# Keeping the MLP pre-activation in bf16 and taking SiLU's slope from one later ScalarE pass

## Chip, cores and metric

One core of a Trainium2 (trn2) chip. The metric is device time in microseconds (us), lower is better.

## The reference, cut to what matters

Two long-convolution blocks `A` and two MLP blocks `B` alternate with residual adds; the outputs are the result and the gradients of all inputs and weights, from one call.

```python
def _B_ref(x, w1, w2):                       # x 2048x448, w1 448x1792, w2 1792x448, all bf16
    h = jnp.einsum("bsd,df->bsf", x, w1)
    h = _silu(h)
    return jnp.einsum("bsf,fd->bsd", h, w2)

x = x + _A_ref(_layernorm(x), k, v, ...)
x = x + _B_ref(_layernorm(x), B_w1, B_w2)    # "layer 0"
x = x + _A_ref(_layernorm(x), k, v, ...)
x = x + _B_ref(_layernorm(x), B_w1, B_w2)    # "layer 1"
# outputs: x and the vjp with grad_out for q, k, v, shift_k, ssm_k, ssm_D, w1, w2
```

The backward of `silu` needs its slope at every one of 2048 x 1792 pre-activations, in both layers.

## The kernel before

The kernel has three parts: a spectral prefix for `A` (to about 107 us), the MLP part (to about 555 us), and a suffix with the backward of `A` and the weight gradients. The MLP part walks over the sequence in four chunks of 512. For each chunk and layer, `h` computes the 1792 hidden features in two halves of seven 128-row tiles; two PSUM buffers `ps_h` take the matmul results in turn.

```python
def h(self, c, L, nT, half, hold):
    aT = self.td.tile([P, NF // 2, 512], BF16, name="aT", tag="T", bufs=3)
    dT = self.td.tile([P, NF // 2, 512], BF16, name="dT", tag="D", bufs=3)
    hold.append((aT, dT))
    for ft0, n in ((0, 2), (2, 2), (4, 2), (6, 1)) if half == 0 else ((7, 1), (8, 2), (10, 2), (12, 2)):
        ps = k.psum.tile([P, 2, 512], FP32, name="ps_h", tag="mm", bufs=2)
        ...                                                       # 4 or 8 matmuls into ps
        nc.scalar.activation(a, ps[:, 0:n, :], ACT.Silu)                      # L543
        nc.scalar.activation(tm, ps[:, 0:n, :], ACT.Tanh, scale=-0.5)         # L544
        wv = ...                                                  # tile w1p, bufs=1
        nc.vector.tensor_scalar(out=wv, in0=tm, scalar1=1.0, scalar2=None, op0=ALU.add)   # L547
        nc.vector.tensor_tensor(out=wv, in0=wv, in1=a, op=ALU.mult)                       # L548
        nc.vector.tensor_tensor(out=tm, in0=wv, in1=tm, op=ALU.subtract)                  # L549
    if L == 1:
        ...                                     # dT = Copy(dT, bias=1.0), four ScalarE pieces
    else:
        nc.gpsimd.dma_start(out=k.DT_d[c, half], in_=dT[:])       # to memory; load_l0 adds the 1.0 later
```

With t = tanh(-x/2), twice the slope is 1 - t + (1 + t) * silu(x); the three VectorE operations form it without the 1, and `rh` (half of `rstd`) takes the factor 2 out again. Other users of VectorE in these loops are the residual adds (`X`), the layer norm's statistics (`ln_st`, `ln_mv`), and the backward reductions `ln_bwd`. VectorE works through one queue, in order: in its timeline, shown below, a slope operation (L548, at 175.13 us) starts only as the 2.02 us residual add that was queued ahead of it (L514, at 173.19 us) ends.

In the suffix, `_wgrad_w2_first` reads activations back with transposing loads, `dstat<-A_d` on SyncE's queue, while GpSimd's queue fetches other large tiles:

```python
        _load_minv(k, nc.gpsimd)                                  # Minvs, 1 MB
        ...                                                       # fft stage 1
        _wgrad_w2_first(k, None, range(10, NF))                   # last transposed loads dstat<-A_d
        ...
            nc.gpsimd.dma_start(out=t[0], in_=k.SPEC_d["K"][:, lo:hi])        # kk_c, 0.5 MB each
            nc.gpsimd.dma_start(out=t[1], in_=k.SPEC_d["KV"][:, lo:hi])
            if cp == 2:
                nc.gpsimd.dma_start(out=ksf[:], in_=_pm(k.KS_d[:]))           # 1.8 MB
```

Of the kernel before, what the change touches and what calls it, by code (L numbers as in the profile page):

```python
# [10 lines left out]
FP32 = mybir.dt.float32  # L11
BF16 = mybir.dt.bfloat16
ACT = mybir.ActivationFunctionType
# [4 lines left out]
P = 128  # L18
S = 2048
D = 448  # L20
# [100 lines left out]
def kernel(  # L121
# [52 lines left out]
    k.Gsb = keep.tile([P, 5, P], BF16, name="Gsb")  # L174
    nc.gpsimd.dma_start(out=k.Gsb[:].rearrange("p a k -> p (a k)"), in_=gs_h.ap())
    k.rstd = [keep.tile([P, J], FP32, name=f"rstd{i}") for i in range(4)]
    k.rh = [keep.tile([P, J], FP32, name=f"rhalf{i}") for i in range(2)]
    k.mhalf = keep.tile([P, 4], FP32, name="mhalf")
    nc.gpsimd.memset(k.mhalf[:], -0.5)
    nc.scalar.activation(k.rh[1][:, 0:4], k.mhalf[:], ACT.Silu)  # L180
    k.wk = ctx.enter_context(tc.tile_pool(name="wk", bufs=1))
    k.dp = ctx.enter_context(tc.tile_pool(name="dp", bufs=1))
    with tc.tile_pool(name="yk", bufs=1, side="right") as yk:
# [275 lines left out]
class Main:  # L459
# [64 lines left out]
    def b_tr(self, n_g):  # L524
        nT = self.ch.tile([P, ND, 512], BF16, name="nT", tag="nT", bufs=2)
        self.transp(n_g, nT, [(DC * i, DC * i + DC) for i in range(4)])
        return nT

    def h(self, c, L, nT, half, hold):
        nc, k = self.nc, self.k  # L530
        aT = self.td.tile([P, NF // 2, 512], BF16, name="aT", tag="T", bufs=3)
# [4 lines that stand above are left out]
            for u in range(n):  # L536
                ft = ft0 + u
                for dc in range(ND):
                    nc.tensor.matmul(ps[:, u, :], lhsT=self.w1sb[:, dc, ft * P:(ft + 1) * P], rhs=nT[:DC, dc, :], start=(dc == 0), stop=(dc == ND - 1))  # L539
            o = ft0 - 7 * half  # L540
            a = aT[:, o:o + n, :]
            tm = dT[:, o:o + n, :]
            nc.scalar.activation(a, ps[:, 0:n, :], ACT.Silu)  # L543
            nc.scalar.activation(tm, ps[:, 0:n, :], ACT.Tanh, scale=-0.5)  # L544
            w = self.ch.tile([P, 2, 512], BF16, name="w1p", tag="w1p", bufs=1)
            wv = w[:, 0:n, :]
            nc.vector.tensor_scalar(out=wv, in0=tm, scalar1=1.0, scalar2=None, op0=ALU.add)  # L547
            nc.vector.tensor_tensor(out=wv, in0=wv, in1=a, op=ALU.mult)  # L548
            nc.vector.tensor_tensor(out=tm, in0=wv, in1=tm, op=ALU.subtract)  # L549
            k.bal.add("act", 1.05 * n)  # L550
            k.bal.add("dve", 0.9 * n)
        if L == 1:
            for o in range(0, 7, 2):
                n = min(2, 7 - o)
                nc.scalar.activation(dT[:, o:o + n, :], dT[:, o:o + n, :], ACT.Copy, bias=1.0)
            k.bal.add("act", 3.4)
        else:
            nc.gpsimd.dma_start(out=k.DT_d[c, half], in_=dT[:])
            self.store_plain(k.A_d[0], aT, c, half)
        if L == 1:  # L560
            self.store_turned(k.A_d[1], aT, c, half)
# [54 lines left out]

    def ln_bwd(self, u0, n_t, cp, g_res, G_out):
        nc = self.nc
        junk = self.ch.tile([P, D], BF16, name="lb_junk", tag="w1p", bufs=1)
        nc.vector.scalar_tensor_tensor(out=junk[:], in0=u0, scalar=1.0, in1=n_t, op0=ALU.mult, op1=ALU.mult, accum_out=cp[:, 1:2])  # L620
        cc = self.ch.tile([P, 2], FP32, name="lb_cc", tag="lb_cc", bufs=2)
        nc.vector.tensor_scalar(out=cc[:], in0=cp, scalar1=-1.0 / D, scalar2=None, op0=ALU.mult)
        nc.vector.scalar_tensor_tensor(out=u0, in0=n_t, scalar=cc[:, 1:2], in1=u0, op0=ALU.mult, op1=ALU.add)  # L623
        nc.vector.scalar_tensor_tensor(out=G_out, in0=u0, scalar=cc[:, 0:1], in1=g_res, op0=ALU.add, op1=ALU.add)  # L624
        self.k.bal.add("dve", 2.0)

    def gn(self, c, L, ghT, nb, gres, na):
# [7 lines left out]
        for tl in range(4):  # L635
            t = 4 * c + tl
            pn = k.psum.tile([P, 512], FP32, name="ps_n", tag="tr" if L == 1 and tl % 2 else "po", bufs=2)
            for ft in range(NF):
                nc.tensor.matmul(pn[:, :D], lhsT=ghT[ft // 7][:, ft % 7, tl * P:(tl + 1) * P], rhs=self.w1T[:, ft, :], start=(ft == 0), stop=(ft == NF - 1))  # L639
            u0 = self.ch.tile([P, D], FP32, name="lb_u0", tag="lb_u0", bufs=2)  # L640
            nc.scalar.activation(u0[:], pn[:, :D], ACT.Identity, scale=k.rh[L][:, t:t + 1], accum_out=cp[:, tl, 0:1])
            k.bal.add("act", 0.75)
            self.ln_bwd(u0[:], nb[:, tl, :], cp[:, tl, :], gres(tl), G[:, t, :])
            if L == 1:
                nc.vector.tensor_tensor(out=gyt[:, tl, :], in0=G[:, t, :], in1=na[:, tl, :], op=ALU.mult)
            else:
                gy = self.ch.tile([P, D], FP32, name="gy", tag="lb_u0", bufs=2)
                nc.vector.tensor_tensor(out=gy[:], in0=G[:, t, :], in1=na[:, tl, :], op=ALU.mult)
                nc.vector.tensor_tensor(out=k.gYb[:, t, :], in0=gy[:], in1=gyt[:, tl, :], op=ALU.add)
            u1 = self.ch.tile([P, D], FP32, name="lb_u1", tag="lb_u0", bufs=2)  # L650
            nc.vector.scalar_tensor_tensor(out=u1[:], in0=G[:, t, :], scalar=k.rstd[si][:, t:t + 1], in1=self.Y[:, t, :], op0=ALU.mult, op1=ALU.mult, accum_out=cp[:, 4 + tl, 0:1])
            k.bal.add("dve", 1.3)
            self.ln_bwd(u1[:], na[:, tl, :], cp[:, 4 + tl, :], G[:, t, :], G[:, t, :])
# [5 lines left out]
    def load_l0(self, c):  # L659
# [3 lines left out]
        for hh in range(2):  # L663
            t = self.td.tile([P, NF // 2, 512], BF16, name="dTl", tag="D", bufs=3)
            i = nc.sync.dma_start(out=t[:], in_=k.DT_d[c, hh])
            if c == 0:
                k.d0_load = i
            for o in range(0, 7, 2):
                n = min(2, 7 - o)
                nc.scalar.activation(t[:, o:o + n, :], t[:, o:o + n, :], ACT.Copy, bias=1.0)  # L670
            k.bal.add("act", 3.2)
            dT.append((None, t))
        nb = self.ch.tile([P, 4, D], BF16, name="nb_l", tag="nb", bufs=2)
        nc.sync.dma_start(out=nb[:], in_=_pm(k.N_d[1][:])[:, sl, :])
# [14 lines left out]
    def run(self):  # L689
# [7 lines left out]
        for c in range(4):  # L697
# [10 lines left out]
            self.h((c + 1) % 4, 0 if c < 3 else 1, nT, 0, fol)  # L708
            self.out(c, cur, False)
            cur = fol  # L710
        nc.vector.tensor_scalar(out=k.rh[0][:], in0=k.rstd[1][:], scalar1=0.5, scalar2=None, op0=ALU.mult)
        for c in range(4):
            gb, gT = self.g_pre(c, 1)
            self.h(c, 1, nT, 1, cur)
            if c < 3:
                na1 = self.a_fwd(c + 1, 2, None)
            nc.vector.tensor_scalar(out=k.rh[1][:, 4 * c:4 * c + 4], in0=k.rstd[3][:, 4 * c:4 * c + 4], scalar1=0.5, scalar2=None, op0=ALU.mult)
            self.out(c, cur, True)
            box = []
            ghT = self.ga(c, 1, gT, cur, (lambda: box.append(self.b_pre(c + 1, 3))) if c < 3 else None)  # L720
# [67 lines left out]
def _wgrad_rest(k, pool, after, mov3):  # L788
# [13 lines left out]
    def fin_w1(ft, ps, aux):  # L802
# [3 lines left out]
        for dc in range(ND):  # L806
            nc.tensor.transpose(pt[:, dc, :], o[:, dc * DC:(dc + 1) * DC], k.ident[:])  # L807
        o7 = pool.tile([DC, ND, P], BF16, name="do7", tag="do7", bufs=2)
        nc.scalar.activation(o7[:], pt[:], ACT.Copy, scale=0.5)  # L809
        nc.gpsimd.dma_start(out=out7v[:, :, ft * P:(ft + 1) * P], in_=o7[:])  # L810

    with k.tc.issue_after(after[-1]):
# [191 lines left out]
```

## Time and profile before

| | before |
|---|---|
| three runs known at the prediction, us | 869.88, 869.68, 858.88 |
| span of the profiled execution | 868.2 us |
| MLP part: first SiLU / first output cast / fourth output cast / last `ps_n` group starts at | 112.03 / 242.22 / 407.98 / 555.57 us |

Those four marks are found in every trace, and the three stretches between them are compared. The first holds all of layer 0's forward and the first chunk's forward in layer 1 (five chunk steps), the second three full chunk steps of layer 1, the third the last backward chunk of layer 1 and layer 0's backward. The stretch table of the kernel before (columns: window, its length, busy us of PE, PEld, DVE, ACT and POOL with counts, granted clock, DMA share, GB/s):

```profile
112.03:242.22 130.19, 122.41 (x639) 57.74 (x638) 112.35 (x253) 107.29 (x135) 33.88 (x39) 1.00 0.61 199
242.22:407.98 165.76, 153.98 (x793) 73.66 (x792) 129.86 (x294) 120.44 (x151) 20.09 (x25) 0.96 0.71 182
```

TensorE (PE) is 94% busy in the first stretch, VectorE (DVE) 86%.

The timeline of VectorE shows how these belong together (start us, duration, engine, line, operation):

```profile
172.99 0.29 DVE L547 TENSOR_SCALAR w1p<-dT 128x512 bf16<-128x512 bf16 x1
173.19 2.02 DVE L514 TENSOR_TENSOR X<-x0c,a_t 128x1792 f32<-128x1792 bf16 x1
175.13 0.42 DVE L548 TENSOR_TENSOR w1p<-w1p,aT 128x512 bf16<-128x512 bf16 x1
175.46 0.62 DVE L256 BATCH_NORM_STATS2 ln_st<-X 128x6 f32<-128x448 f32 x1
176.00 0.41 DVE L549 TENSOR_TENSOR dT<-w1p,dT 128x512 bf16<-128x512 bf16 x1
```

Slope operations and the next chunk's residual add and statistics stand in one queue with no gap, so each slope operation ahead of them pushes back the statistics, and with them the normalization of the next chunk (L270), for which TensorE waited 2.9 us in this stretch.

### The profile page before, as it was taken

How to read it: one execution, taken by the hardware profiler on the slowest of the kernel's cores; microseconds unless marked ns; L12 is line 12 of the kernel's file. 1: busy time of each engine (PE TensorE's matmuls, PEld its weight loads, DVE VectorE, ACT ScalarE, POOL GpSimd, SP SyncE). 2: the span in 40 equal slices, each digit the busy share in tenths (PEclk: the TensorE clock that was granted, in tenths of full speed). 3: DMA queues.
4: the chain of work that ended last, by engine and by line, in shares of the span. 5: the costliest groups of instructions: out<-in, count | busy, mean ns of one | idle time of the engine just before them, and what ended most of it. 6: DMA issues, size and time to landing. Idle time of an engine off the chain costs nothing.

```text
span 868.2 us, 12830 instructions
## 1 busy us (share of the span) xinstructions
PE 755.6 (87%) x4924; PEld 410.3 (47%) x4924; DVE 565.7 (65%) x1201; ACT 481.9 (56%) x598; POOL 145.7 (17%) x218
## 2 busy tenths in 40 slices
PE   6997699999999899897978879993579896989997
PEld 4975434444444344343433334451346564545553
DVE  4789778898938969779387989962166632760100
ACT  5789678787968585788666654232145433330010
POOL 1143222322110120110000101111111121221010
PEclk9999899999999899899989999997799998999999
DMA  9279895455667576596795654999988879987771
GB/s 324 99 234 271 304 261 193 176 207 212 149 175 169 166 176 168 154 245 192 178 254 174 232 153 136 225 257 227 200 293 291 267 276 244 125 231 175 185 186 44
DMA packets 168392, 178.60 MB, mean 206 GB/s; under 512 B 135374, under 2 KB 139086, under 8 KB 167308
## 3 DMA queue, kind: packets, MB, share of 16 engines
q1 hardware_dynamic: 144304, 81.70, 39.6%
q0 software_dynamic: 21696, 88.07, 31.7%
q10 hardware_dynamic: 2332, 8.03, 3.1%
q8 instruction: 38, 0.62, 0.3%
q14 instruction: 22, 0.18, 0.1%
HBM read 66.64 MB, written 70.65 MB: 158 GB/s over the span
## 4 chain that ended last, share of the span: by engine, by line
DVE 25%; DMA 21%; issue 20%; PE 16%; ACT 14%; POOL 4%; ACTq 0%; SPq 0%; POOLq 0%; DVEq 0%
DMA dstat<-A_d 4%; PE ps_d L773 4%; DMA xsw_c<-Zg 3%; DVE lb_u L623 3%; DVE X L624 2%; DMA GY_d<-gyt 2%; DVE lb_junk L620 2%; DMA out_dram<-gKD 2%; PE ps_g L598 2%; DVE dT L549 2%; DVE w1p L548 2%; DVE ghT L607 2%; PE ps_h L539 2%; ACT ghp L602 2%; ACT aT L543 2%
## 5 line engine op out<-in xcount | busy, mean ns | idle before, releaser
L773 PEld LDWEIGHTS <-dstat 128*128 128x128 bf16 x896 | 87.0, 98 | 104.9 <-DMA dstat<-A_d 24.7
L598 PE MATMUL ps_g<-gT,w2T 128*128 128x512 bf16 x448 | 110.8, 398 | 20.3 <-ACT ghp L602 17.1
L773 PE MATMUL ps_d<-mov,dstat 128*128 128x448 bf16 x448 | 95.6, 357 | 23.9 <-DMA dstat<-A_d 23.9
L539 PE MATMUL ps_h<-nT,w1sb 112*128 112x512 bf16 x448 | 106.7, 384 | 6.3 <-ACT dT L544 4.6
L639 PE MATMUL ps_n<-w1T,ghT 128*128 128x448 bf16 x448 | 94.5, 358 | 10.0 <-DVE ghT L607 6.9
L773 PE MATMUL ps_d<-dmov,dstat 128*128 128x448 bf16 x448 | 94.6, 353 | 4.7 <-DMA dmov<-N_d 2.9
L569 PE MATMUL ps_o<-w2sb,aT 128*128 128x448 bf16 x448 | 92.6, 352 | 1.4 <-DVE X L570 1.3
L598 PEld LDWEIGHTS <-w2T 128*128 128x128 bf16 x448 | 45.4, 101 | 78.6 <-issue 33.6
L602 ACT CAST ghp<-ps_g 128x1024 bf16<-128x1024 f32 x56 | 56.4, 1007 | 35.8 <-PE ps_g L598 14.4
L539 PEld LDWEIGHTS <-w1sb 112*128 112x128 bf16 x448 | 43.7, 98 | 62.5 <-issue 18.3
L639 PEld LDWEIGHTS <-ghT 128*128 128x128 bf16 x448 | 43.4, 99 | 56.4 <-DVE ghT L607 11.0
L543 ACT ACTIVATE aT<-ps_h 128x1024 bf16<-128x1024 f32 (+1 forms) x64 | 59.2, 925 | 9.3 <-PE ps_h L539 5.1
L569 PEld LDWEIGHTS <-aT 128*128 128x128 bf16 x448 | 42.5, 98 | 42.5 <-ACT aT L543 3.0
L544 ACT ACTIVATE dT<-ps_h 128x1024 bf16<-128x1024 f32 (+1 forms) x64 | 59.4, 928 | 0.0
L804 DVE CAST dout<-ps_d 128x448 bf16<-128x448 f32 x14 | 8.7, 624 | 75.6 <-PE ps_d L773 75.6
L809 ACT ACTIVATE do<-ps_dt 112x512 bf16<-112x512 bf16 x14 | 8.4, 598 | 74.9 <-PE ps_dt L807 74.9
L228 PE MATMUL ps_v<-Gsb,pa 128*128 128x128 bf16 x336 | 43.7, 223 | 5.5 <-DVE Zg L113 3.2
L229 PE MATMUL ps_v<-Gsb,pb 128*128 128x128 bf16 x336 | 42.6, 223 | 5.3 <-DVE pb L884 2.7
L547 DVE TENSOR_SCALAR w1p<-dT 128x1024 bf16<-128x1024 bf16 (+1 forms) x64 | 26.5, 415 | 23.7 <-ACT dT L544 22.1
L229 PEld LDWEIGHTS <-pb 128*128 128x128 bf16 x336 | 33.0, 100 | 15.5 <-DVE pb L438 6.0
L548 DVE TENSOR_TENSOR w1p<-w1p,aT 128x1024 bf16<-128x1024 bf16 (+1 forms) x64 | 39.6, 619 | 1.0
L549 DVE TENSOR_TENSOR dT<-w1p,dT 128x1024 bf16<-128x1024 bf16 (+1 forms) x64 | 39.5, 618 | 1.0
(184 smaller groups left out, 1311.6 us busy)
## 6 DMA issues: line engine op xcount, KB each, us to landing
A_d<-aT POOLq DMA_DIRECT2D x8, 896.0 KB, 5.5
DT_d<-dT POOLq DMA_DIRECT2D x8, 896.0 KB, 4.2
A_d<-turned POOLq DMA_DIRECT2D x8, 896.0 KB, 4.8
GH_d<-turned POOLq DMA_DIRECT2D x8, 896.0 KB, 7.3
dTl<-DT_d SPq DMA_DIRECT2D x8, 896.0 KB, 6.0
GH_d<-ghT POOLq DMA_DIRECT2D x8, 896.0 KB, 8.2
dstat<-A_d SPq DMA_DIRECT2D x14, 512.0 KB, 6.4
dstat<-GH_d SPq DMA_DIRECT2D x14, 512.0 KB, 3.8
```

The costliest lines, as they stand in the source:

```text
L228: nc.tensor.matmul(pv[:, i, :], lhsT=pa[:, i * P:(i + 1) * P], rhs=k.Gsb[:, ga, :], start=True, stop=False)
L229: nc.tensor.matmul(pv[:, i, :], lhsT=pb[:, i * P:(i + 1) * P], rhs=k.Gsb[:, gb, :], start=False, stop=True)
L539: nc.tensor.matmul(ps[:, u, :], lhsT=self.w1sb[:, dc, ft * P:(ft + 1) * P], rhs=nT[:DC, dc, :], start=(dc == 0), stop=(dc == ND - 1))
L543: nc.scalar.activation(a, ps[:, 0:n, :], ACT.Silu)
L544: nc.scalar.activation(tm, ps[:, 0:n, :], ACT.Tanh, scale=-0.5)
L548: nc.vector.tensor_tensor(out=wv, in0=wv, in1=a, op=ALU.mult)
L549: nc.vector.tensor_tensor(out=tm, in0=wv, in1=tm, op=ALU.subtract)
L569: nc.tensor.matmul(po[:, :D], lhsT=aT[ft // 7][0][:, ft % 7, tl * P:(tl + 1) * P], rhs=self.w2sb[:, ft, :], start=(ft == 0), stop=(ft == N ...
L598: nc.tensor.matmul(ps[:, u, :], lhsT=self.w2T[:, b, ft * P:(ft + 1) * P], rhs=gT[:, b, :], start=(b == 0), stop=(b == ND - 1))
L602: nc.scalar.copy(gh[:], ps[:])
L639: nc.tensor.matmul(pn[:, :D], lhsT=ghT[ft // 7][:, ft % 7, tl * P:(tl + 1) * P], rhs=self.w1T[:, ft, :], start=(ft == 0), stop=(ft == NF - 1))
L773: nc.tensor.matmul(ps[:, :D], lhsT=st[:, t, :], rhs=movs[gi][:, t, :], start=(gi == 0 and t == 0), stop=(gi == len(groups) - 1 and t == NT ...
```

## The change

The intent: do not compute the slope in four steps at the place where SiLU is computed and a fifth one later. Evict the pre-activation x itself to bf16 in the place of Tanh, and apply ScalarE's `Derivative_silu` to it in the later pass that so far only added 1.0. The diff, cut to its core:

```diff
+    def slope(self, d):
+        for o in range(0, 7, 2):
+            n = min(2, 7 - o)
+            self.nc.scalar.activation(d[:, o:o + n, :], d[:, o:o + n, :], ACT.Derivative_silu)
 ...
             nc.scalar.activation(a, ps[:, 0:n, :], ACT.Silu)
-            nc.scalar.activation(tm, ps[:, 0:n, :], ACT.Tanh, scale=-0.5)
-            w = self.ch.tile([P, 2, 512], BF16, name="w1p", tag="w1p", bufs=1)
-            ...                                  # the three VectorE operations
+            e = nc.scalar if o == 4 else nc.vector
+            _copy(nc, e, tm, ps[:, 0:n, :])
         if L == 1:
-            ...                                  # the Copy pass with bias=1.0
+            if half == 1:
+                for _, d in hold:
+                    self.slope(d)
 ...
-        junk = self.ch.tile([P, D], BF16, name="lb_junk", tag="w1p", bufs=1)
+        junk = self.ch.tile([P, D], BF16, name="lb_junk", tag="lb_junk", bufs=1)
 ...                                              # load_l0: Copy pass -> self.slope(t); halved scales undone
```

More of the change, by code (lines that the diff above doesn't have):

```diff
@@ L176 @@
     k.rstd = [keep.tile([P, J], FP32, name=f"rstd{i}") for i in range(4)]
-    k.rh = [keep.tile([P, J], FP32, name=f"rhalf{i}") for i in range(2)]
+    k.warm = keep.tile([P, 4], FP32, name="warm")
     k.mhalf = keep.tile([P, 4], FP32, name="mhalf")
     nc.gpsimd.memset(k.mhalf[:], -0.5)
-    nc.scalar.activation(k.rh[1][:, 0:4], k.mhalf[:], ACT.Silu)
+    nc.scalar.activation(k.warm[:], k.mhalf[:], ACT.Silu)
     k.wk = ctx.enter_context(tc.tile_pool(name="wk", bufs=1))
@@ L527, in b_tr @@
         return nT
+    def slope(self, d):
+        for o in range(0, 7, 2):
+            n = min(2, 7 - o)
+            self.nc.scalar.activation(d[:, o:o + n, :], d[:, o:o + n, :], ACT.Derivative_silu)
+        self.k.bal.add("act", 3.4)
     def h(self, c, L, nT, half, hold):
@@ L543, in h @@
             nc.scalar.activation(a, ps[:, 0:n, :], ACT.Silu)
-            nc.scalar.activation(tm, ps[:, 0:n, :], ACT.Tanh, scale=-0.5)
-            w = self.ch.tile([P, 2, 512], BF16, name="w1p", tag="w1p", bufs=1)
-            wv = w[:, 0:n, :]
-            nc.vector.tensor_scalar(out=wv, in0=tm, scalar1=1.0, scalar2=None, op0=ALU.add)
-            nc.vector.tensor_tensor(out=wv, in0=wv, in1=a, op=ALU.mult)
-            nc.vector.tensor_tensor(out=tm, in0=wv, in1=tm, op=ALU.subtract)
-            k.bal.add("act", 1.05 * n)
-            k.bal.add("dve", 0.9 * n)
+            e = nc.scalar if o == 4 else nc.vector
+            _copy(nc, e, tm, ps[:, 0:n, :])
+            k.bal.add("act", 0.52 * n)
+            k.bal.add(*(("act", 0.52 * n) if e is nc.scalar else ("dve", 0.6 * n)))
         if L == 1:
-            for o in range(0, 7, 2):
-                n = min(2, 7 - o)
-                nc.scalar.activation(dT[:, o:o + n, :], dT[:, o:o + n, :], ACT.Copy, bias=1.0)
-            k.bal.add("act", 3.4)
+            if half == 1:
+                for _, d in hold:
+                    self.slope(d)
         else:
@@ L640, in gn @@
             u0 = self.ch.tile([P, D], FP32, name="lb_u0", tag="lb_u0", bufs=2)
-            nc.scalar.activation(u0[:], pn[:, :D], ACT.Identity, scale=k.rh[L][:, t:t + 1], accum_out=cp[:, tl, 0:1])
+            nc.scalar.activation(u0[:], pn[:, :D], ACT.Identity, scale=k.rstd[2 * L + 1][:, t:t + 1], accum_out=cp[:, tl, 0:1])
             k.bal.add("act", 0.75)
@@ L667, in load_l0 @@
                 k.d0_load = i
-            for o in range(0, 7, 2):
-                n = min(2, 7 - o)
-                nc.scalar.activation(t[:, o:o + n, :], t[:, o:o + n, :], ACT.Copy, bias=1.0)
-            k.bal.add("act", 3.2)
+            self.slope(t)
             dT.append((None, t))
@@ L710, in run @@
             cur = fol
-        nc.vector.tensor_scalar(out=k.rh[0][:], in0=k.rstd[1][:], scalar1=0.5, scalar2=None, op0=ALU.mult)
         for c in range(4):
@@ L716, in run @@
                 na1 = self.a_fwd(c + 1, 2, None)
-            nc.vector.tensor_scalar(out=k.rh[1][:, 4 * c:4 * c + 4], in0=k.rstd[3][:, 4 * c:4 * c + 4], scalar1=0.5, scalar2=None, op0=ALU.mult)
             self.out(c, cur, True)
@@ L808, in fin_w1 @@
         o7 = pool.tile([DC, ND, P], BF16, name="do7", tag="do7", bufs=2)
-        nc.scalar.activation(o7[:], pt[:], ACT.Copy, scale=0.5)
+        nc.scalar.copy(o7[:], pt[:])
         nc.gpsimd.dma_start(out=out7v[:, :, ft * P:(ft + 1) * P], in_=o7[:])
```

## The prediction

> **What bounds the kernel now.** I read the page first (busy shares, slices), then the groups of instructions, the table of windows, the waits by window, and the timeline of ScalarE and VectorE for the MLP part. The page says:
>
> ```profile
> PE 755.6 (87%) x4924; PEld 410.3 (47%) x4924; DVE 565.7 (65%) x1201; ACT 481.9 (56%) x598; POOL 145.7 (17%) x218
> ...
> PE   6997699999999899897978879993579896989997
> DVE  4789778898938969779387989962166632760100
> ACT  5789678787968585788666654232145433330010
> ```
>
> TensorE is the busiest engine. A slice is 21.7 us; the MLP code that changes runs from about 107 us (slice 5) to 515 us (slice 23), and the edited forward function `h` only from 112 to 396 us. So nothing after slice 24 changes; it can only move earlier or later as a block. By stretch (columns: busy us of PE, PEld, DVE, ACT, POOL, then granted clock, DMA share, GB/s):
>
> ```profile
> 165.00:190.00 25.00, 23.49 (x122) 10.98 (x122) 22.16 (x51) 21.05 (x28) 6.01 (x8) 1.00 0.54 199
> 290.00:345.00 55.00, 51.18 (x257) 24.12 (x256) 45.93 (x108) 40.29 (x52) 7.42 (x10) 0.94 0.68 175
> 435.00:480.00 45.00, 36.87 (x188) 17.32 (x186) 35.42 (x84) 29.37 (x39) 2.46 (x3) 0.92 0.68 198
> ```
>
> The first row is one chunk of layer 0 (forward), the second one chunk of layer 1 (forward and backward), the third mostly layer 0's backward. In the first two TensorE is 93 to 94% busy, with VectorE at 89% and 84%, ScalarE at 84% and 73%. In the waits, TensorE seldom waits for `h`'s consumers:
>
> ```profile
> PE ps_h L539 <- ACT dT L544: 2.8, 3, 1.0
> ...
> PE ps_n L639 <- DVE ghT L607: 3.1, 1, 3.1
> ```
>
> (total us, times, longest; the first from 107 to 225 us, the second from 290 to 345 us.) How much could be won at all? In the chain eight 512-column matmuls take 1.73 us, 0.216 each; in the timeline 54 of 448 columns take 10.38 us, 0.19 each. A layer-0 chunk needs 56 of each, 12.1 + 10.6 us, and about 1.5 of transposes: 24; the chunks follow each other in 24.8 to 27 us (starts of the normalization: 155.5, 180.3, 207.3). A layer-1 chunk needs twice that, about 48 us; its period is 56.4 us (output cast at 299.3 and at 355.6), of which the granted clock of 0.94 explains some 3. So at most some 2 us per layer-0 chunk and 5 to 8 per layer-1 chunk are not TensorE's own work.
>
> **What the Trainium skill says.** (1) "ScalarE: Activation LUTs", section What ACT_TABLE_LOAD costs: every function costs the same per element; a switch to a function of another table set costs a load of 1283 ns and a drain of about 1380 ns. The trace agrees as far as it goes: one load in the whole execution, at the start,
>
> ```profile
> L544 ACT ACTIVATE dT<-ps_h 128x1024 bf16<-128x1024 f32 (+1 forms) x64 | 59.4, 928 | 0.0
> L543 ACT ACTIVATE aT<-ps_h 128x1024 bf16<-128x1024 f32 (+1 forms) x64 | 59.2, 925 | 9.3 <-PE ps_h L539 5.1 <-issue 2.9 <-ACT na L270 0.2
> ...
> L180 ACT ACT_TABLE_LOAD x1 | 1.3, 1283 | 1.2 <-PEq L988 1.2
> ```
>
> and Tanh (L544) as long as SiLU (L543). So SiLU, Tanh, Copy and Identity share a set here; whether the derivative is in it no line shows. (2) "PSUM — Partial Sum Buffer", section PSUM bank collisions raise a hardware error: two engines must not read one bank at the same time. The trace agrees that such readers go one after the other: where both evict one tile of two banks in the prefix, VectorE waited for ScalarE each time:
>
> ```profile
>   ACT KB L111: 1.4, 4
> ```
>
> (3) "VectorE: DVE Perf Modes", section The perf-mode tier table: a PSUM source drops a tier, fp32 to 1x. Here a 1024-wide VectorE eviction of fp32 PSUM takes 1215 ns, the 1024-wide SBUF operation L547 456 ns.
>
> **The change, part by part.** Removed on VectorE, all between 112 and 405 us:
>
> ```profile
> L547 DVE TENSOR_SCALAR w1p<-dT 128x1024 bf16<-128x1024 bf16 (+1 forms) x64 | 26.5, 415 | 23.7 <-ACT dT L544 22.1
> ...
> L548 DVE TENSOR_TENSOR w1p<-w1p,aT 128x1024 bf16<-128x1024 bf16 (+1 forms) x64 | 39.6, 619 | 1.0
> L549 DVE TENSOR_TENSOR dT<-w1p,dT 128x1024 bf16<-128x1024 bf16 (+1 forms) x64 | 39.5, 618 | 1.0
> ```
>
> VectorE loses 26.5 + 39.6 + 39.5 = 105.6 us, ScalarE 59.4 us of Tanh. Added: 64 evictions of the pre-activation. Per half 0 one 1024-wide one is on ScalarE (8 in all, by 1.01 us of the like cast L602: 8.1 us); VectorE gets two 1024-wide and one 512-wide per half 0, three and one per half 1: 40 x 1.215 + 16 x 0.69 (the 448-wide one takes 0.62; 64 columns more) = 59.6 us. Net: **VectorE -46 us, ScalarE -51 us**, some 6 us of each in every one of the 8 chunk steps (4 chunks, 2 layers). The 64 later Copy passes (29.8 + 28.8 us) become 64 derivative passes of the same shapes: by (1) no change but for table loads. The halved scales save five tiny VectorE operations, 0.7 us; the private junk tile takes one false dependence away between backward reductions and `h`.
>
> Table loads: had the derivative been in SiLU's set, the natural edit would have been to put it in Tanh's place, straight from PSUM, without VectorE and without a later pass. That it is deferred, and in layer 1 until both halves' SiLUs are done, tells me (about 85%) that it is in another set. In program order that makes 4 switches there and 3 back: 7 x 2.66 = 18.6 us of ScalarE (an estimate from (1)).
>
> **What lies on the path.** Two effects oppose. (a) In layer 1 VectorE's in-order queue is full from 268 to 294 us with the backward reductions, so that the slope of half 1 is finished only around 302 us, after the residual add (L514) has waited for a store; TensorE's 3.1 us wait above is this. The slopes now need only a 1.2 us eviction, and ScalarE has a hole for them:
>
> ```profile
> ACT na L270 <- issue: 7.4, 1, 7.4
> ```
>
> A pass over both halves is 6 x 1.06 + 2 x 0.63 = 7.6 us, with a load and drain 10.2: it overhangs the hole by 2 to 3 us, but the 3.5 us of half-1 copies that now sit between L602's evictions are gone. I count -2 to -3 us for each of three chunks and -1 for the last, whose half-0 slopes also come late. (b) The release of a `ps_h` buffer, of which there are two, was SiLU + Tanh, 1.94 us on ScalarE alone; it becomes SiLU, then VectorE, 1.0 + 0.1 + 1.2 = 2.3 us, plus whatever stands in VectorE's queue (up to 2.0 us of L514). TensorE fills a buffer in 8 x 0.216 = 1.73 us, so two buffers give a period of (1.73 + 1.94)/2 = 1.84 us before and 2.0 us or more after when nothing else is interleaved. Against it: other matmuls are interleaved, and both engines have 6 us more air per chunk. For layer 0 I count -0.5 us per chunk, -2 in all. Sum: -2 (layer 0) - 8 (layer 1) + 1 (loads that show) = -9 us; the rest of the program starts earlier by that: **861 us**.
>
> **The rivals.** *The PSUM wait takes the place of the removed one:* in layer 1 half 1's evictions stand behind up to 25 us of backward reductions (before, L547 of half 1 came at 290.6 us for SiLUs of 274 to 283 us, which then held no PSUM), and TensorE stops with both buffers full. For it: VectorE's 84 to 89%. Against: the total of VectorE's work falls by 13%. It would cost 3 to 6 us per layer-1 chunk and give some 870 to 880. *ScalarE switches tables more than 7 times:* the trace has instructions ahead of their program order (the next chunk's L270 before the first SiLU), so slopes of half 0 could be slipped between SiLUs of half 1; up to 4 more pairs per chunk would be 4 x 4 x 5.3 = 85 us of ScalarE, of which its freed 51 us hide most: 875 to 910. *VectorE and ScalarE were the real limit:* then nearly all of the 46 us over 8 chunk steps would show, limited by the slack of TensorE, 2 x 4 + 7 x 4 = 36 us: 835 to 850. The waits of only a few us speak against it.
>
> **Range and chances.** The first rival at half strength and the second in a mild form lift the result to about 878; recovering two thirds of layer 1's slack gives about 846. The three runs before already lie 11 us apart, which alone is 1.3%. Faster than 852 by a 2% margin 0.20, within 2% 0.69, slower than 887 0.11.
>
> **What would show it.** Right: ScalarE near 430 us plus 9 to 19 of table work, VectorE near 520; 8 table loads in the page's groups (2 would mean one set, more than 10 the second rival); no ScalarE hole before L270 in layer 1; the TensorE wait for ghT gone; period of a layer-1 chunk near 54 us. Wrong: TensorE waiting for VectorE's eviction of `ps_h` more than 10 us in all (first rival); the MLP stretch unchanged while both engines idle (then a DMA or TensorE alone bounded it); or a tail after 560 us that waits for the same transfers and gives the gain back.

## More of the kernel before

The chain of waits of that same window, which the prediction did not ask for, says something else:

```profile
by line: issue 15.0%; DVE w1p L548 8.0%; DVE dT L549 7.8%; ACT nb L270 6.9%; DVE w1p L547 6.8%; DVE ln_st L256 6.0%; ACT aT L543 5.6%; POOL rstd L263 5.4%; PE ps_h L539 5.1%; ACT dT L544 5.0%; DVE X L514 4.5%; PE ps_o L569 3.6%; ACT na L270
```

Followed back from its end, 22.6% of the stretch goes through the three VectorE operations (L547 6.8, L548 8.0, L549 7.8), 10.5% more through VectorE's statistics and residual add, and the two lines of matmuls that it lists have 8.7%.

## The result and the profile after

| | runs | lowest | median | highest | mean |
|---|---|---|---|---|---|
| before | 6 | 858.88 | 863.64 | 869.88 | 864.4 |
| after | 6 | 835.22 | 845.80 | 868.83 | 848.4 |

Ratios in this text are the mean time of one kernel's fast runs over that of the other's of the same rounds, so not quite the ratio of the medians quoted. Here it is 0.9676, interval 0.96 to 0.9753: faster by over 2%, where 861 us and "within 2%" had been predicted as most likely. But a run counts as fast only within 1.5% of the fastest of its kernel: the changed kernel ran 835, 837 and 837, and also 854, 858 and 869. The ratio compares the three quick ones with all six of the kernel before. Over all runs the difference of the medians is 17.8 us, of the means 16.0. Both profiled executions (868.2 and 867.0 us) lie at the long end of their kernels and are of nearly equal length. So the first question to the traces is where 17 us were won, and the second where they went in that execution. The page of the changed kernel, in the same order as shown for before:

```profile
PE 753.6 (87%) x4894; PEld 411.7 (47%) x4924; DVE 527.9 (61%) x1060; ACT 478.0 (55%) x573; POOL 143.0 (16%) x218
...
PE   6998699999999999999779899950579996999997
DVE  5789668777349788682779899730156631760100
ACT  5789566669879798998566552230136532330010
```

From slice 5 to 18 TensorE is at 9 nearly throughout; and there is a hole (5 0 5) in slices 26 to 28. The stretch table, with the hole as its third row:

```profile
113.75:235.68 121.93, 119.94 (x633) 58.27 (x633) 89.04 (x165) 88.66 (x107) 31.49 (x39) 1.00 0.63 205
235.68:389.69 154.01, 146.77 (x768) 71.19 (x773) 118.52 (x247) 134.32 (x154) 19.16 (x25) 1.00 0.78 190
...
577.00:615.00 38.00, 0.13 (x1) 0.13 (x2) 0.35 (x1) 0.22 (x1) 0.55 (x1) 0.52 1.19 108
```

| stretch | before | after | difference |
|---|---|---|---|
| layer 0 and first chunk of layer 1, forward | 130.2 | 121.9 | -8.3 |
| layer 1, three chunk steps | 165.8 | 154.0 | -11.8 |
| end of layer 1 and backward of layer 0 | 147.6 | 148.9 | +1.3 |
| sum | 443.5 | 424.9 | **-18.7** |

The marks stand on ScalarE's work, and TensorE is not at the same matmul at each of them: the weight loads (PEld) between the marks number 638, 792 and 621 before and 633, 773 and 644 after. At about 0.2 us a matmul (an estimate from the matmul times in the prediction), the three differences are some -7, -8 and -3 us work for work. The sum is not touched by this (2051 and 2050 weight loads).

In the first stretch TensorE goes from 94% to 98% busy and VectorE from 86% to 73%. The saved 8.3 us are 5.8 of idle time (7.8 to 2.0) and 2.5 of busy time, some of the latter being six matmuls fewer between the marks (639 to 633). The Trainium skill warns against this measure ("Perfetto Trace Analysis", section Identifying the Most-Contended Engine: matmul busy share is not a good measure of how close a kernel is to its limit; the share of the weight loads is better). The trace agrees: weight loads took 57.74 of 130.19 us, 44%, and 58.27 of 121.93, 48%. The chain of the same stretch is now led by matmuls, with TensorE's own lines `ps_o` and `ps_h` at 32%:

```profile
by line: PE ps_o L570 20.5%; PE ps_h L545 11.9%; DVE dT L113 5.5%; ACT aT L549 4.8%; ACT nb L270 4.7%; DVE ln_st L256 3.5%; ACT nT L111 3.1%; DVE X L571 2.2%; issue 2.2%; ACT na L270 2.1%; ACT L549 2.1%; DVE X L514 1.6%; ACT gT L111 1.2%; A
```

The added work, from the groups of VectorE and ScalarE, and the waits of TensorE in the first stretch, after and then before:

```profile
L113 DVE CAST dT<-ps_h 128x1024 bf16<-128x1024 f32 (+1 forms) x56 | 59.2, 1065 | 31.7 <-ACT aT L549 31.6
L532 ACT ACT_TABLE_LOAD x16 | 20.5, 1283 | 0.3
L549 ACT ACT_TABLE_LOAD x15 | 19.2, 1283 | 0.2
```

```profile
PE ps_h L545 <- DVE dT L113: 0.7, 3, 0.3
PE ps_h L545 <- ACT nT L111: 0.5, 1, 0.5
PE ps_t L501 <- ACT nb L270: 0.3, 1, 0.3
```

```profile
PE ps_h L539 <- ACT dT L544: 3.2, 4, 1.0
PE ps_t L501 <- ACT nb L270: 2.9, 3, 1.3
PE ps_o L569 <- DVE X L570: 1.3, 1, 1.3
```

The 56 evictions on VectorE took 59.2 us (predicted 59.6). With the one at the start, there are 32 table loads, not 8. And where TensorE waited 2.9 us for the normalization and 3.2 for Tanh in this stretch before, it now waits 0.3 us for the first and 0.7 us for the evictions that took Tanh's place.

In the suffix the two profiled executions meet again at about 617 us. The waits of TensorE from 530 to 640 us, before:

```profile
PE ps_d L773 <- DMA dstat<-A_d: 23.9, 2, 23.2
```

and after:

```profile
PE ps_d L769 <- DMA dstat<-A_d: 39.0, 2, 38.3
```

The last transposed loads of `A_d` hold TensorE for 23.2 us before and 38.3 us after; 15 of the MLP's gain are lost there in this execution. In the hole the granted clock reads 0.52 while TensorE stands still, so a long wait lowers the mean clock of the core. The first two MLP stretches hardly differ between slow and fast executions: a slow one of the changed kernel, 865.9 us, had 122.0, 154.1 and 148.9 us, and two fast ones of variants with the same MLP code, 844.2 and 850.5 us, had 121.9, 153.3 and 146.3, and 121.9, 153.6 and 149.8 us. So the stretches may be compared between executions, the third only to some 3.5 us, and total times may not.

### The profile page after: what moved, and what is told of

It reads as the page before. It is cut to its first block, busy times and chain, and to the rows that moved or that the text cites. A ratio compares the mean times of both kernels' runs of the same rounds, so it can differ in the third digit from the quotient of the medians.

```text
span 867.0 us, 12590 instructions
## 1 busy us (share of the span) xinstructions
PE 753.6 (87%) x4894; PEld 411.7 (47%) x4924; DVE 527.9 (61%) x1060; ACT 478.0 (55%) x573; POOL 143.0 (16%) x218
## 4 chain that ended last, share of the span: by engine, by line
DVE 18%; DMA 18%; issue 17%; PE 16%; ACT 10%; POOL 2%; POOLq 0%; ACTq 0%; SPq 0%; DVEq 0%
DMA dstat<-A_d 6%; PE ps_d L769 6%; PE ps_o L570 3%; DVE dT L113 3%; DVE lb_u L624 2%; DVE X L625 2%; DMA dTl<-DT_d 2%; ACT ghp L603 2%; DVE lb_junk L621 2%; PE ps_h L545 2%; DMA out_dram<-gKD 2%; PE ps_n L640 2%; DVE ghT L608 2%; DMA dmov<-in_grad_out_dram 2%; DMA xsw_c<-Zg 1%
## 5 line engine op out<-in xcount | busy, mean ns | idle before, releaser
L599 PE MATMUL ps_g<-gT,w2T 128*128 128x512 bf16 x431 | 104.7, 388 | 17.3 <-ACT ghp L603 16.3
L769 PE MATMUL ps_d<-dmov,dstat 128*128 128x448 bf16 x448 | 97.1, 360 | 4.6 <-DMA dmov<-N_d 2.2
L113 DVE CAST dT<-ps_h 128x1024 bf16<-128x1024 f32 (+1 forms) x56 | 59.2, 1065 | 31.7 <-ACT aT L549 31.6
L805 ACT COPY do<-ps_dt 112x512 bf16<-112x512 bf16 x14 | 8.2, 586 | 75.1 <-PE ps_dt L803 75.1
L532 ACT ACTIVATE dTl<-dTl 128x1024 bf16<-128x1024 bf16 (+1 forms) x32 | 28.7, 947 | 18.2 <-DMA dTl<-DT_d 18.2
L608 DVE TENSOR_TENSOR ghT<-dT,ghp 128x1024 bf16<-128x1024 bf16 (+1 forms) x32 | 19.6, 622 | 31.0 <-ACT ghp L603 31.0
L113 DVE COPY Zg<-ps_tr 128x2048 bf16<-128x2048 bf16 x5 | 6.0, 1222 | 51.0 <-DMA W2P_d<-dpo 47.4
```

Of the source, the lines that this page charges most:

```text
L113: eng.tensor_copy(out, in_)
L532: self.nc.scalar.activation(d[:, o:o + n, :], d[:, o:o + n, :], ACT.Derivative_silu)
L599: nc.tensor.matmul(ps[:, u, :], lhsT=self.w2T[:, b, ft * P:(ft + 1) * P], rhs=gT[:, b, :], start=(b == 0), stop=(b == ND - 1))
L608: nc.vector.tensor_tensor(out=ghT[hh][:, o:o + len(u), :], in0=dT[hh][1][:, o:o + len(u), :], in1=gh[:, u[0]:u[0] + len(u), :], op=ALU.mult)
L769: nc.tensor.matmul(ps[:, :D], lhsT=st[:, t, :], rhs=movs[gi][:, t, :], start=(gi == 0 and t == 0), stop=(gi == len(groups) - 1 and t == NT ...
```

## The experiments

Two theories stood at the start. **Own gain:** the change saves some 18 us in the MLP part, because VectorE's in-order queue (or ScalarE's) was the real limit; the rest of the 28 us is chance in the tail. **Tail:** the change mainly moves the suffix's transfers relative to each other, and its gain is a better or worse collision there. All runs gave the reference's results unless a wrong result is noted.

### 1. The changed kernel again, unchanged

> The changed kernel, not altered, to see how its executions fall. In its first profile (867 us, a slow one) the MLP part had gained 17 us by the last ps_n matmul (538.6 against 555.6 us), and then TensorE stood 38 us for the transposed loads of A_d (23 us in the profile of before), so both kernels were level again at 617 us. Theory A: the executions of 835 to 837 us are those in which this one wait is short (about 6 us), and everything else agrees to 2 us; the profile of a fast execution will show it. Theory B: the clock is granted lower all over in the slow ones, and all stretches stretch alike. Expected from A: times spread from 835 to 869 in no more than a few clusters, mean near 848.

Measured on another chip: 837.69 to 870.61, mean 853.4, against 857.2 to 880.9, mean 872.1, for eleven runs of before (ratio 0.9781, interval 0.9656 to 0.9905). The two modes recur: 838 once, 847 to 853 three times, 866 to 871 twice. The MLP stretches are the same to 0.1 us. The wait for `dstat<-A_d` was 26.7 us. So the 3.2% was not repeated; some 2% was, and against a mark of 2% this series is unclear.

### 2. and 3. Before and after, with two large loads moved behind the second `kk_c` load

```diff
-        _load_minv(k, nc.gpsimd)                 # at the start of the suffix
 ...
+                if cp == 1:
+                    with tc.issue_after(i0.ins):  # i0: the second kk_c load
+                        _load_minv(k, nc.gpsimd)
                 if cp == 2:
-                    nc.gpsimd.dma_start(out=ksf[:], in_=_pm(k.KS_d[:]))
+                    with tc.issue_after(i0.ins):
+                        nc.gpsimd.dma_start(out=ksf[:], in_=_pm(k.KS_d[:]))
```

> The kernel before, with the loads of Minvs (1 MB) and ksf (1.8 MB) held behind the second kk_c load, so that they no longer run beside the last transposed loads of A_d. Theory A (these loads collide with the transposed ones and make the wait of 23 us): the wait falls under 10 us, the spread of times shrinks from 11 us to under 4, and the median falls to 845 to 852. Theory B (the wait is the transposed loads' own time, or the clock): no change over 1%.

> The changed kernel with the same two loads held back. Theory A: spread under 4 us, time 828 to 836, and the difference to before_dma is the gain of the MLP part alone, 17 us (2.0%), not the 28 us that the verdict's fast runs show. Theory B: still two clusters 20 to 30 us apart.

Measured: before so edited 866.7 to 883.8, median 868.9 (ratio to before 1.0063, 0.9978 to 1.0147), where some 850 had been expected; after so edited 845.2 to 856.0, median 851.9 (0.9876, 0.9795 to 0.9957), where 828 to 836 had been expected. The long wait for a transposed load was shorter (4.6 us after, 12.2 before, where under 10 had been expected), and so was the scatter of the changed kernel (10.8 us between its extremes instead of 33); before so edited still had 17.1, and under 4 had been expected for both. But the moved loads now ran beside the spectral part, which took 83 us after so edited, instead of 70, and 80 before; that is the likely reason why both expected times missed. The difference between the two medians, 17.0 us, is what the own-gain theory said.

### 4. The order of the slope pass enforced

```diff
-            nc.scalar.activation(a, ps[:, 0:n, :], ACT.Silu)
+            si = nc.scalar.activation(a, ps[:, 0:n, :], ACT.Silu)
 ...
+                with self.tc.issue_after(si.ins):
                     for _, d in hold:
                         self.slope(d)
```

> The changed kernel with the slope pass held behind the last SiLU of its chunk, as in program order: 8 table loads in place of 32. If the 24 additional loads (1.28 us each, 31 us of ScalarE) cost time on the path, the MLP part ends 5 to 10 us earlier than in the changed kernel; if they lie in ScalarE's idle time, as the 4.7 us shorter layer-1 period suggests, it ends within 3 us of it, and perhaps later, because all 7.6 us of slopes then stand in one block before the evictions of ps_g.

The changed kernel has 32 table loads because its instructions do not stand on ScalarE in the order of the program text: single slopes are slipped between SiLUs. From its timeline of ScalarE:

```profile
204.54 1.02 ACT L549 ACTIVATE aT<-ps_h 128x1024 bf16<-128x1024 f32 x1 [0.65 <-PE ps_h L545]
205.59 1.28 ACT L532 ACT_TABLE_LOAD   x1
206.88 1.06 ACT L532 ACTIVATE dT<-dT 128x1024 bf16<-128x1024 bf16 x1
207.94 1.28 ACT L549 ACT_TABLE_LOAD   x1
209.23 1.02 ACT L549 ACTIVATE aT<-ps_h 128x1024 bf16<-128x1024 f32 x1
```

Held behind the last SiLU, the passes need only these loads beside the one at the start (eight in all had been expected, it is ten):

```profile
L532 ACT ACT_TABLE_LOAD x5 | 6.4, 1283 | 0.1
L549 ACT ACT_TABLE_LOAD x4 | 5.1, 1283 | 0.1
```

Time: 836.4 to 853.8, median 849.2, mean 846.9 (ratio 0.9749, 0.9626 to 0.9871), beside 849.7 and 853.4 for the unchanged one. The MLP part took 429.2 us, against 424.9 with 32 loads: 4.3 us longer, where the forecasts had been 5 to 10 us shorter, or within 3 us. Twenty-two loads, 28 us of ScalarE, were taken away, and no time was won. The edit also puts all slopes in one late block, so what the loads alone cost on the path is not separated.

### 5. and 6. Before, without Tanh or without the three VectorE operations

Each removes one engine's half of the old slope; both give wrong gradients (relative error 0.050 and 0.075, in the gradient of w1).

```diff
 # without Tanh: VectorE's operations read SiLU's output instead
-            nc.scalar.activation(tm, ps[:, 0:n, :], ACT.Tanh, scale=-0.5)
-            nc.vector.tensor_scalar(out=wv, in0=tm, ...)
+            nc.vector.tensor_scalar(out=wv, in0=a, ...)
-            nc.vector.tensor_tensor(out=tm, in0=wv, in1=tm, op=ALU.subtract)
+            nc.vector.tensor_tensor(out=tm, in0=wv, in1=a, op=ALU.subtract)
 # without VectorE: Tanh stays, tile w1p and L547 to L549 go, and with them
-            k.bal.add("dve", 0.9 * n)
```

> The kernel before without the Tanh: the three VectorE operations read the SiLU output instead (wrong result on purpose), so 59.4 us of ScalarE go, VectorE's work stays, and a ps_h buffer is free after SiLU alone. Read from the trace, not from the time: the stretch from the first SiLU to the first output cast is 130.2 us before and 121.9 after the change, from there to the fourth cast 165.8 and 154.0. Theory P (the early release of ps_h and the freed ScalarE give the gain): this kernel shows most of it, 123 us and 157 us. Theory V (VectorE's in-order queue gives it): 128 to 130 and 162 to 166.

> The kernel before with the Tanh but without the three VectorE operations behind it (wrong result on purpose): 105.6 us of VectorE go, ScalarE and the release of ps_h stay, and the backward junk tile no longer shares a buffer with w1p. Theory V: most of the gain is here, 123 us for the first stretch and 154 or less for the second. Theory P: 128 to 130 and 162 to 166.

| MLP stretches, us | layer 0 | layer 1 | backward of 0 | sum | against before |
|---|---|---|---|---|---|
| before | 130.2 | 165.8 | 147.6 | 443.5 | |
| without Tanh | 125.0 | 161.1 | 148.7 | 434.8 | -8.8 |
| without the three VectorE operations | 120.9 | 157.8 | 146.3 | 425.0 | **-18.5** |
| the change | 121.9 | 154.0 | 148.9 | 424.9 | -18.7 |

Totals were 878.8 and 840.2 in one look each (before on the same chip: 866.2); the first is the longer one, although its MLP part is shorter, because its wait for `dstat<-A_d` was 33.4 us against 10.2. For the mechanism only the stretches count. Without Tanh they lie between the forecasts of the two theories; without the three VectorE operations the first is as theory V had it, and the second, 157.8, is above its 154. In sum the removal of the VectorE operations gives the gain of the whole change, and that of Tanh less than half. The first stretch without the VectorE operations, then without Tanh:

```profile
113.20:234.07 120.87, 119.19 (x634) 58.41 (x633) 70.20 (x165) 81.95 (x102) 31.76 (x39) 1.00 0.66 215
115.28:240.24 124.96, 120.78 (x634) 58.03 (x633) 110.17 (x253) 76.26 (x95) 33.39 (x39) 0.99 0.60 198
```

Without the VectorE operations TensorE is 98.6% busy, and its wait for Tanh falls from 3.2 to 0.2 us although Tanh is still there. But this is not VectorE relieved alone. With the three operations the edit removes their line `k.bal.add("dve", ...)`, and the balancer that deals out small work by these counts now gives VectorE normalizations and copies (`na`, `nb`, `nT`, `gT`) that ScalarE did before: ScalarE's busy time in this stretch falls from 107.3 to 82.0 us along with VectorE's from 112.4 to 70.2, and a piece of the normalization takes 0.50 us on VectorE where it took 0.75 on ScalarE. What the pair does show: without Tanh ScalarE loses even more (107.3 to 76.3 us), and the stretch only 5.2 us instead of 9.3. So the relief of ScalarE is not enough for the gain, and the rest, some 4 us of this stretch by that difference (an estimate), needs less slope work on VectorE, or the moved pieces. A run with the balancer's choices held fixed was not made. The two gains are not simply additive: either relieves the same chain of SiLU, Tanh, slope, statistics and normalization.

### 7. All evictions of the changed kernel on ScalarE

```diff
-            e = nc.scalar if o == 4 else nc.vector
+            e = nc.scalar
```

> The changed kernel with all evictions of the pre-activation on ScalarE, none on VectorE: ScalarE gets 56 x 0.92 = 52 us back (as much as Tanh had), VectorE loses 59 us more, and ps_h is released as in the kernel before. Theory P: it loses most of the gain of the first stretch, 128 to 130 us. Theory V: as the changed kernel or better, 120 to 122 us. The rival of the prediction (evictions stuck in VectorE's queue) would make it faster in layer 1 than the changed kernel, under 150 us for the second stretch.

It was to separate "two engines hand the PSUM buffer on" from "VectorE has less to do". The MLP stretches were 121.3, 155.8 and 145.5 us: 422.6 us, 2.3 us less than the change. That difference comes from the third stretch, which varies by as much between executions with the same MLP code, and is not shown to be the edit's. The first stretch is as theory V had it; the second is not under 150 us, as it would have been if evictions stuck in VectorE's queue had cost the change much in layer 1. First stretch:

```profile
114.70:236.04 121.34, 119.71 (x634) 58.69 (x633) 69.69 (x162) 91.47 (x109) 31.39 (x39) 0.99 0.63 204
```

VectorE is busy 19 us less here than in the changed kernel and the stretch is 0.6 us shorter: TensorE was already the limit there. The balancer moved work from ScalarE to VectorE in this run too, so that ScalarE is busy only 3 us more. The total was 861.1 in one look, with 37.1 us of waiting for `dstat<-A_d`.

### 8. The derivative in Tanh's place, straight from PSUM

```diff
-            e = nc.scalar if o == 4 else nc.vector
-            _copy(nc, e, tm, ps[:, 0:n, :])
+            nc.scalar.activation(tm, ps[:, 0:n, :], ACT.Derivative_silu)
 ...                                              # no later pass
```

> The edit that the prediction called natural: the derivative straight from PSUM in Tanh's place, no eviction, no VectorE operation, no later pass. It needs a table load before nearly every activation of h, about 128 of 1.283 us = 164 us of ScalarE against 58 of later passes saved. If loads cost what they measured in the changed kernel (1.28 us each, no 1.38 us of drain before them), a group of h takes 4.5 us of ScalarE against 1.7 us of TensorE: 64 groups x 4.5 = 288 us, so the two stretches together grow from 276 to 330 us or more, and the kernel takes 890 to 930 us.

Correct, and 917.7 us. SiLU and its derivative are in different table sets, so each of 64 groups pays two loads (128 in all):

```profile
118.92 1.02 ACT L549 ACTIVATE aT<-ps_h 128x1024 bf16<-128x1024 f32 x1
119.96 1.28 ACT L550 ACT_TABLE_LOAD   x1
121.26 1.02 ACT L550 ACTIVATE dT<-ps_h 128x1024 bf16<-128x1024 f32 x1
122.30 1.28 ACT L549 ACT_TABLE_LOAD   x1
123.59 1.02 ACT L549 ACTIVATE aT<-ps_h 128x1024 bf16<-128x1024 f32 x1
```

A group takes 1.02 + 1.28 + 1.02 + 1.28 = 4.6 us of ScalarE, and the MLP part 502 us instead of 424.9: here ScalarE is the bound. The Trainium skill's rule to batch activations by table set ("ScalarE: Activation LUTs", section Table sets: the hidden batching unit) holds where the loads are on the path, as here (96 more loads than the change are 123 us more of ScalarE, and the MLP part is 77 us longer); in experiment 4 keeping to it won no time, though the order of the slopes changed there too.

### 9. to 12. A quiet tail

The loads that had been moved wrongly in 2 and 3 were put on SyncE's queue, behind the last transposed load and before the plain loads that are needed later. These two no longer run beside the transposed loads then, and are under way before they are needed.

```diff
-        _load_minv(k, nc.gpsimd)
 ...
         _wgrad_w2_first(k, None, range(10, NF))
+        with tc.issue_after(last_tr):             # last_tr: the last transposed load
+            _load_minv(k, nc.sync)
+            nc.sync.dma_start(out=ksf[:], in_=_pm(k.KS_d[:]))
 ...
-                if cp == 2:
-                    nc.gpsimd.dma_start(out=ksf[:], in_=_pm(k.KS_d[:]))
 ...
+        with tc.issue_after(last_tr):
             _wgrad_rest(k, dp2, after, mov3)
```

> The kernel before with another order of the loads around the wait for the transposed A_d tiles: on the SyncE queue the last three transposed loads go first, and the plain loads of A_d (3 x 0.5 MB), Minvs (1 MB) and ksf (1.8 MB) behind them, still ahead of the spectral part, which the first attempt (before_dma, after_dma) disturbed. If the collision is the cause of the scatter: TensorE's longest wait for dstat under 6 us, spread of times under 8 us, median 850 to 856. If it is the transposed loads' own time: as the kernel before, 857 to 881.

> The changed kernel with the same order of loads. Collision theory: spread under 8 us, median 833 to 838, and the mean of all its executions is 17 to 19 us (2.0 to 2.2%) under that of before_tail: the gain of the MLP part and nothing else. If the verdict's 28 us of the first comparison were the change's own, the difference is 25 us or more.

With it went experiment 7's edit, with and without this tail:

> All pre-activation evictions on ScalarE and the same order of loads: the MLP part is 2.3 us shorter than in the changed kernel in the trace (422.6 against 424.9 us from the first SiLU to the last ps_n). Expected 831 to 836, 1 to 3 us under after_tail; if not, the 2.3 us are lost in the tail.

> All pre-activation evictions on ScalarE, timed, without the new order of loads. VectorE's queue was the limit, so this is not slower than the changed kernel: mean of all executions within 1% of that of after_again relative to the kernel before (0.98), with the same wide scatter (836 to 868).

| same chip | lowest | median | highest | ratio to before |
|---|---|---|---|---|
| before (11 runs) | 855.7 | 862.4 | 894.9 | |
| before, quiet tail | 858.1 | 863.2 | 866.5 | 1.0037 (0.9978 to 1.0096) |
| after, quiet tail | 839.6 | 844.1 | 844.8 | 0.9806 (0.9754 to 0.9858) |
| evictions on ScalarE | 854.8 | 864.5 | 872.1 | 1.0002 (0.9917 to 1.0087) |
| evictions on ScalarE, quiet tail | 837.1 | **840.8** | 845.9 | 0.9768 (0.9711 to 0.9826) |

The quiet tail still left one wait of some 10 us, for a later plain load of `A_d` (under 6 had been expected), its spectral part took 83 us before and 88 after, instead of 70, and it did not make any kernel as quick as had been expected (850 to 856, 833 to 838, and 831 to 836 with the evictions on ScalarE). But it reduced the scatter: 8.4 and 5.2 us between the extremes, where before had 39 in this series and the changed kernel 34 and 33 in its two, on other chips. The change is then worth 863.2 - 844.1 = 19.1 us of the medians, 19.9 of the means, 2.3%; the scatter of the six and six runs leaves some 3 us either way. The MLP parts of the two profiled executions, both fast, took 441.2 and 421.5 us, 19.7 us apart: the gain is all there. And the plain version of experiment 7, expected to run as the changed kernel does, ran like the kernel before, while the same edit with the quiet tail is 24 us quicker. The waits of TensorE between 530 and 640 us, first of that plain version, then of the changed kernel with quiet tail:

```profile
PE ps_d L769 <- DMA dstat<-A_d: 47.6, 1, 47.6
```

```profile
PE ps_d L769 <- DMA dstat<-A_d: 12.5, 3, 10.3
```

That this wait is what scatters shows in all nine traces with the old order of loads: the span after the MLP part, less the waits for `dstat<-A_d`, is 284 to 295 us in each, while these waits come to 8 to 48 us. So a kernel whose MLP part is 20 us shorter than that of before can end no earlier than it, because one wait in the suffix is as much longer. The correct version with the lowest median here has the evictions on ScalarE and the quiet tail: 840.8 us (the changed kernel with the old tail was not run in this series). Its lead of 3.3 us over the changed kernel with quiet tail is not shown to be the edit's: their intervals overlap, and the MLP parts of their profiled executions took 422.0 and 421.5 us.

## Why the prediction was wrong, point by point

**The size.** The predicted 861 was 869.7, the median of three, less 9. Six runs of before had a median of 863.6: 6 us of the miss is that base. The other 9.7 is the gain, put at 9 and 18.7 in the traces. Then 863.6 - 18.7 = 844.9, beside 845.8 measured. That the two meet so closely is luck in part, for the six runs behind 845.8 lie 34 us apart.

| term of the sum | predicted | measured between the marks | work for work, about |
|---|---|---|---|
| layer 0 | -2 | -8.3 | -7 |
| layer 1, and the table loads that show | -8 + 1 | -11.8 | -8 |
| layer 0's backward | 0 | +1.3 | -3 |

The rows do not cut the chunks exactly as the prediction did: the first stretch includes one chunk's forward of layer 1, and the third the last backward chunk of layer 1. The sums compare.

**The step that failed** is effect (b), "For layer 0 I count -0.5 us per chunk", and with it the reason against the third rival, "The waits of only a few us speak against it". The slack had been read correctly: 24 us of TensorE's own work per layer-0 chunk, and after the change a chunk step takes 121.93 / 5 = 24.4 us. But the prediction took only a quarter of the slack of 2 us, because it looked for the waits that name `h`'s consumers, such as the 2.8 us for Tanh. What the runs showed in its place: nearly all of the slack came back, 1.7 us a step, because the slope work of VectorE and ScalarE had held up more than `ps_h`. VectorE's queue delayed residual adds, statistics and normalization of the next chunk, and TensorE's waits for these (2.9 us for the normalization, 1.3 for a residual add) went as well. Every run that took slope work off both engines had the first stretch at 121 to 122 us (experiments 4, 6 and 7); relief of ScalarE alone, which also frees `ps_h` sooner, gave 5.2 us instead of 8.3 (experiment 5). So the third rival, which named both engines and put "835 to 850", was the right one. How the gain divides between the two is not shown. The -7 us for layer 1 were nearly right.

**Effect (a)** was right in kind: TensorE's wait of 3.1 us for `ghT` is no longer among its waits of layer 1, the ScalarE hole before L270 is gone too (16.1 us of such waits of `na` from 107 to 400 us before, 0.5 after), and a chunk step of layer 1 went from 56.4 to 51.75 us (from one output cast to the next, 299.26 to 355.62 before and 289.28 to 341.03 after). Predicted was 54. In that step the granted clock read 0.93 before and 1.00 after; how much of the 4.6 us is the clock's is not separated. In the kernel before with quiet tail the same step took 56.0 us at 0.95.

**The first rival**, waiting for VectorE's eviction of `ps_h`, is false: 0.7 us in the first stretch and 0.2 in layer 1, where the rival had placed it; over 10 was named as its sign. VectorE did wait for ScalarE to finish with a buffer (31.6 us in the group of evictions), as the Trainium skill ("PSUM — Partial Sum Buffer", section PSUM bank collisions raise a hardware error) let one expect, but VectorE had the time. The line that the prediction showed for this rule does not bear on it: in the code ScalarE and VectorE read different halves of that tile of two banks, so a shared bank is not shown to be why VectorE waited there.

**The second rival** came true in its ordering and false in its cost: 31 loads after the first instead of 7, 39.7 us of ScalarE, and an order with 22 fewer of them was no quicker. The prediction's inference that the derivative is in another table set was right, experiment 8 shows it.

**Totals of engines:** VectorE 527.9 (about 520 predicted); ScalarE 478.0, of which the loads are 41, so 437 of other work (430 predicted).

**The last sign of being wrong**, "a tail after 560 us that waits for the same transfers and gives the gain back", did occur: in some executions of every kernel with the old tail, and in full in the plain version of experiment 7. The median of the changed kernel escaped most of it.

**What stays open:** what makes the wait for `dstat<-A_d` short in one execution and long in the next. Plain loads beside the transposed ones are not enough: in the trace of experiment 4 the same loads stand beside them, Minvs landed in 9 us instead of 36, and the longest wait was 4.4 us. No execution of the unchanged changed kernel near 835 us was caught by the profiler, so that its wait is short there is inferred from the variants. The share of VectorE and of ScalarE in the gain stays open, because the balancer moved work in experiments 6 and 7. How much of the gain is due to the private tile for `lb_junk` was not separated: the kernel before with such a tile beside `w1p` does not fit into SBUF. Experiment 6 keeps the shared tag but has no `w1p` any more, so it bears on both. In the first stretch the tile can have no part: its first use before is at 269.5 us.

## What to carry to other kernels

An engine that is "94% busy" can still be held up by another: ask for the chain of waits in the window of the stage that changes, and see whose lines it passes through, before counting only the waits that name the changed lines. When an experiment takes work away, check the busy time of every engine in the stretch: a program that balances its own load may have moved other work. Work in an in-order queue delays everything behind it, also what belongs to the next chunk. And when runs of one kernel scatter more than the gain in question, compare stage by stage in the traces and make the scattering part quiet in both kernels, before believing a ratio.

## What the Trainium skill lacked or had wrong

- "ScalarE: Activation LUTs", What ACT_TABLE_LOAD costs: the load of 1283 ns agrees in every load of these traces; the drain of about 1380 ns beside it was not seen. The load starts 0.03 us after the operation before it ends and the next activation 0.01 us after it (204.54 + 1.02, 205.59 + 1.28, 206.88). Taking 2.66 us for a switch, as the prediction did, doubles the cost.
- The same page, Table sets: the hidden batching unit, lists no set for the derivative of SiLU. The runs show that it is not in the set of SiLU (128 loads when the two alternate). And the rule says nothing of when a load costs time on the path: the order with 32 loads was no slower than the one with 10 (MLP part 424.9 and 429.2 us).
- "DMA: Bandwidth & Descriptors", Rules for kernel authors: "A transpose next to ordinary DMAs needs nothing" is about correctness. For speed these runs suggest that it can need something: in the first profile of the changed kernel, with plain loads of 1 MB, 1.8 MB and some of 0.5 MB beside the last transposed loads, the DMA engines were busy throughout (share 1.19 in the trace's measure) and moved 108 GB/s for 38 us, while TensorE stood still; with the first two moved behind them the longest wait left was 10.3 us, and times scattered by 5 us instead of 33. It is not so each time: with the old order the longest wait was 4.4 us in the trace of experiment 4.
